# RWKV recurrence, Fourier mixing and MLP on one core: Fourier products folded twice along the features, a list scheduler with insertion, and key transposes by DMA

## The chip, the cores and the metric

The program runs on one core of a Trainium2 chip. Its engines are TensorE (PE, with its weight loads shown apart as PEld), VectorE (DVE), ScalarE (ACT), GpSimd (POOL) and SyncE (SP), each with a queue of its own that is worked through in order; 16 DMA engines move data for all of them. The metric is the device time of one execution in microseconds, lower is better. The three runs before the change took 211.9, 212.37 and 209.75 us (median 211.9).

## What is computed

The inputs r, k, v have the shape (4 batches, 8 heads, 768 steps, 48 features), w and u are (8, 48), and the MLP has weights of 384x1536 and 1536x384. All inputs and the output are float32.

```
for t in range(S):                       # per batch and head, state is 48x48
    y[t]  = r[t] @ (state + (u*k[t]) v[t]^T)
    state = w[:,None]*state + k[t] v[t]^T
x = y with the heads side by side        # (4, 768, 384)
u  = x + real(fft(fft(x, axis=1), axis=2))
un = (u - mean(u)) / sqrt(var(u) + 1e-6) # over the 384 features
out = u + relu(un @ w_ch1) @ w_ch2
```

## The kernel before

**Attention.** Each batch is cut into six chunks of 128 steps, 24 chunks in all (index i; q = i mod 6). For each chunk SP loads k, r (tile `kr`) and v (`vt`), lines 295 to 301. DVE scales k and r by powers of the decay into `KR` (L317), ACT casts v into `V` (L322), PE turns KR in eight 128x128 transposes (`tp`, L327), ACT copies the result out of PSUM (`KRT`, L330), PE multiplies keys and queries (`A_ps`, L341), and two masks give `MA` (ACT copy L353 with a GpSimd select L355, or one DVE multiplication, L348). PE also updates the state (`u_ps`, L369 and L372, DVE copy L376), multiplies queries and state (L396), and sums the masked rows into `yd` (L411). The bonus term u goes its own way: DVE forms `PR` (L331), PE sums it over the features (L391), ACT copies 8 numbers per step (`DE`, L401), GpSimd scales V by them (`TT`, L402), and DVE adds that to `yd` while it writes `X` (L415).

**Fourier part.** Per batch, `fold` (L425) adds and subtracts the two halves of the sequence (`EO`, L433), then the two halves of the features (`XF`, L439). `first` (L457) multiplies by cosine and sine tables over 384 steps: per batch 6 groups of three matmuls of 386 or 384 columns (L463), copied out by ACT (`TT2`, printed as TT, L470). `rev` (L478) copies it backwards into `TR` for the second half of the steps. `second` (L487) multiplies along the features, for each of six blocks of 128 steps two matmuls of 384 columns and four of 192 (L498, L500, L502). DVE adds X (`UF`, L508), and takes mean and variance (L513, L515). Three operations on ACT and DVE give the inverse deviation (square root L524, reciprocal L526, L528), ACT writes the normalised `UN` (L533). `UN` is turned into `UNT` by PE and DVE for batch 0 (L554, L557) and by a DMA transpose on SP for the other batches (L545).

**MLP.** Each batch has two halves of 384 steps (hf 0 to 7). For each half, 12 groups of three matmuls of 384 columns with W1 (L582), a rectifier on ACT (`HT`, L586), and for three blocks of 128 steps 12 matmuls with W2 (L598). DVE adds UF (`osb`, L605), and GpSimd issues the store (L608). W1 and W2 are loaded by six DMAs that GpSimd issues (L638), W1 once the fourth chunk's TT has been issued, W2 once the eighth's has.

**Order.** All work is handed to `_Schedule` (L74) as operations with an estimated duration, what they read and write, and a priority. `order` (L100) goes through time: it takes, over all engines, the operation that can start first, ties by priority, and never puts an operation ahead of one that it has placed. PSUM is divided by name: two banks for A_ps, one each for tp, u_ps and yd, and a ring of three (named "mm") for all Fourier and MLP products. Matmuls of zeros (L614) fill PE's idle time up to an estimated 46 us.

## Time and profile before

| | before |
|---|---|
| runs | 211.9, 212.37, 209.75 us |
| profiled execution, its own time | 211.41 us |
| its span | 209.7 us |
| mean granted TensorE clock | 0.958 |
| busy: PE, DVE, ACT, POOL | 186.7, 136.0, 129.5, 64.0 us |
| HBM read, written | 20.32 MB, 4.72 MB |

The profile covers one execution. The span is the time between the first and the last instruction on the core; the execution's own time is 1.7 us longer. Busy time of PE counts matmuls from start to modelled end, and consecutive ones overlap, so what a stream of matmuls costs is read from the distance between their starts. Views used below: the page (shares and 40 slices), groups of instructions by line, the timeline (start, duration, instruction, and in brackets the idle time ahead of it with what ended it), the chain that ended last (start, duration, piece), and tables by stretch.

### The profile page before, as it was taken

Reading aid. Unit: us, or ns where it says so; the run is one execution under the profiler, and the core shown is the slowest. Engines: PE = TensorE matmul, PEld = TensorE weight load, DVE = VectorE, ACT = ScalarE, POOL = GpSimd, SP = SyncE. Lnnn points to the kernel's source line nnn. Section 1 sums busy time; section 2 is a strip of 40 time slices with the busy share of each in tenths; the row PEclk is TensorE's granted clock in tenths of the full one; section 3 lists DMA queues with packets and bytes.
Section 4 is the critical chain, followed back from the end, with each engine's and each line's share of the span. In section 5 each row is a group of like instructions: output and inputs, shape, how many; then the busy total and the mean of one; then the engine's idle time right before and its main releaser. Section 6 shows DMA issues by size and latency. Waiting matters only on the chain.

```text
span 209.7 us, 4438 instructions
## 1 busy us (share of the span) xinstructions
PE 186.7 (89%) x1729; PEld 118.7 (57%) x1731; DVE 136.0 (65%) x281; ACT 129.5 (62%) x260; POOL 64.0 (31%) x92
## 2 busy tenths in 40 slices
PE   7199975599999699999789999999999999999990
PEld 2056643267576366577457567666567665666550
DVE  5178999649999448899897999883739511111221
ACT  3467852562898686874678986987371895364300
POOL 5017793111038244442344323234110121121131
PEclk9969998569999999999969999999999999999999
DMA  5999999999759999967567000044110144112122
GB/s 103 181 188 190 258 219 210 182 191 172 125 106 164 193 179 219 219 131 150 113 144 150 12 3 0 30 104 94 41 38 0 42 99 126 38 41 75 38 75 75
DMA packets 86548, 24.73 MB, mean 118 GB/s; under 512 B 82944, under 2 KB 84608, under 8 KB 86528
## 3 DMA queue, kind: packets, MB, share of 16 engines
q1 hardware_dynamic: 82848, 17.37, 47.4%
q0 software_dynamic: 3680, 7.08, 13.3%
q8 instruction: 13, 0.21, 0.5%
q14 instruction: 7, 0.06, 0.1%
HBM read 20.32 MB, written 4.72 MB: 119 GB/s over the span
## 4 chain that ended last, share of the span: by engine, by line
PE 37%; issue 27%; DVE 11%; DMA 11%; POOL 6%; ACT 3%; SPq 2%; POOLq 0%; ACTq 0%; DVEq 0%
PE mm L598 7%; DMA vt<-in_v_dram 6%; PE mm L582 5%; DMA kr<-in_r_dram 5%; PE mm L614 4%; PE tp L327 4%; POOL out_dram L608 4%; PE mm L463 3%; DVE KR L317 3%; PE mm L498 3%; PE A_ps L341 2%; PE u_ps L369 2%; DVE XF L439 2%; DVE X L415 1%; PE yd_ps L411 1%
## 5 line engine op out<-in xcount | busy, mean ns | idle before, releaser
L586 ACT ACTIVATE HT<-mm 128x384 bf16<-128x384 f32 x96 | 45.9, 493 | 22.5 <-PE mm L582 22.1
L582 PE MATMUL mm<-UNT,W 128*128 128x384 bf16 x288 | 53.7, 330 | 0.5 <-DVE osb L605 0.3
L598 PE MATMUL mm<-W,HT 128*128 128x384 bf16 x288 | 51.1, 326 | 0.0
L605 DVE TENSOR_TENSOR osb<-mm,UF 128x384 f32<-128x384 f32 x24 | 13.3, 555 | 37.9 <-PE mm L598 37.9
L598 PEld LDWEIGHTS <-HT 128*128 128x128 bf16 x288 | 27.7, 98 | 17.6
L582 PEld LDWEIGHTS <-W 128*128 128x128 bf16 x288 | 27.3, 99 | 17.5 <-issue 1.4
L355 POOL TENSOR_SCALAR_AFFINE_SELECT MA<-AC 128x512 bf16<-128x512 bf16 x29 | 19.4, 676 | 50.4 <-ACT AC L353 49.3
L402 POOL TENSOR_TENSOR TT<-V,DE 128x384 bf16<-128x384 bf16 x24 | 25.0, 1040 | 27.7 <-ACT DE L401 27.0
L608 POOL DMA_DIRECT2D out_dram<-osb x24 | 13.3, 554 | 62.6 <-DVE osb L605 57.6
L317 DVE TENSOR_TENSOR KR<-kr,wtab 128x768 bf16<-128x768 f32 x24 | 24.9, 1044 | 8.6 <-ACT wtab L244 5.7
L330 ACT COPY KRT<-tp 128x1024 bf16<-128x1024 bf16 x24 | 24.5, 1019 | 6.2 <-PE tp L327 6.0
L353 ACT CAST AC<-A_ps 128x512 bf16<-128x512 f32 x29 | 16.6, 591 | 11.7 <-PE A_ps L341 11.7
L614 PE MATMUL mm<-zero 128*128 128x512 bf16 x71 | 20.1, 423 | 1.4 <-DVE wuc L233 1.3
L327 PE MATMUL tp<-ident,KR 128*128 128x128 bf16 x192 | 15.7, 229 | 5.8 <-DVE KR L317 5.6
L322 ACT CAST V<-vt 128x384 bf16<-128x384 f32 x24 | 12.0, 522 | 8.9 <-DMA vt<-in_v_dram 5.1
L327 PEld LDWEIGHTS <-KR 128*128 128x128 bf16 x192 | 12.4, 103 | 9.1 <-DVE KR L317 6.4
L533 ACT ACTIVATE UN<-UF,nm,rstd 128x384 bf16<-128x384 f32 x24 | 15.7, 699 | 2.8 <-DVE nm L528 2.8
L415 DVE TENSOR_TENSOR X<-yd_ps,TT 128x384 bf16<-128x384 f32 x24 | 13.1, 546 | 5.7 <-POOL TT L402 5.7
L470 ACT CAST TT<-mm 128x386 bf16<-128x386 f32 (+1 forms) x24 | 12.7, 600 | 4.3 <-PE mm L463 4.3
L331 DVE TENSOR_TENSOR PR<-KRT 128x512 bf16<-128x512 bf16 x24 | 14.1, 596 | 0.5 <-ACT KRT L330 0.4
L508 DVE TENSOR_TENSOR UF<-mm,X 128x384 f32<-128x384 f32 x24 | 12.7, 551 | 1.8 <-PE mm L502 1.1
L348 DVE TENSOR_TENSOR MA<-A_ps,mtri 128x512 bf16<-128x512 f32 x19 | 12.9, 681 | 1.1 <-PE A_ps L341 1.0
(67 smaller groups left out, 239.6 us busy)
## 6 DMA issues: line engine op xcount, KB each, us to landing
kr<-in_k_dram SPq DMA_DIRECT2D x24, 192.0 KB, 4.5
kr<-in_r_dram SPq DMA_DIRECT2D x24, 192.0 KB, 4.6
vt<-in_v_dram SPq DMA_DIRECT2D x24, 192.0 KB, 4.4
out_dram<-osb POOLq DMA_DIRECT2D x24, 192.0 KB, 2.2
W<-in_moe_w_ch_dram POOLq DMA_DIRECT2D x6, 384.0 KB, 7.7
hid_t<-hid_c SPq DMA_DIRECT2D x1, 576.0 KB, 5.1
te_t<-te_c SPq DMA_DIRECT2D x1, 289.5 KB, 4.3
to_t<-to_c SPq DMA_DIRECT2D x1, 288.0 KB, 4.0
```

Source lines behind the costliest of these rows:

```text
L317: op("DVE", 960, lambda: nc.vector.tensor_tensor(out=KR().rearrange("t s p (a d) -> t (s p) a d", a=2)[:, :, :, 0:D], in0=kr().rearrange(" ...
L327: nc.tensor.transpose(tp()[:, s, p, :], KR()[:, s, p, :], ident)
L330: op("ACT", 1010, lambda: nc.scalar.copy(KRT(), tp()), r=[("tp", i)], w=[("KRT", i)], new=[KRT], use=[tp], pri=pri)
L353: op("ACT", 590, lambda: nc.scalar.copy(AC(), A_ps[a]()), r=[("A", i)], w=[("AC", i, a)], new=[AC], use=[A_ps[a]], pri=pri)
L355: op("POOL", 680, lambda: nc.gpsimd.affine_select(out=MA[a](), in_=AC(), pattern=[[0, NP], [1, 128]], base=0, channel_multiplier=-1, compa ...
L402: op("POOL", 850, lambda: nc.gpsimd.tensor_tensor(out=TT(), in0=V(), in1=DE().unsqueeze(2).to_broadcast([128, H, D]), op=AluOp.mult), r=[( ...
L533: op("ACT", 705, lambda: nc.scalar.activation(out=UN()[:, j, :], in_=UF()[:, j, :], func=Act.Identity, scale=rstd()[:, j:j + 1], bias=nm() ...
L582: nc.tensor.matmul(hp(), lhsT=W1[:, dt, ft * 128:(ft + 1) * 128], rhs=UNT()[:, :, dt, :], start=(dt == 0), stop=(dt == 2))
L586: op("ACT", 490, lambda: nc.scalar.activation(out=HT()[:, ft, :], in_=hp(), func=Act.Relu), r=[("hp", hf, ft)], w=[("HT", hf, ft)], new=[H ...
L598: nc.tensor.matmul(mo(), lhsT=HT()[:, ft, j * 128:(j + 1) * 128], rhs=W2[:, ft, :], start=(ft == 0), stop=(ft == 11))
L608: op("POOL", 550, lambda: nc.gpsimd.dma_start(out=out[b, row:row + 128, :], in_=osb()), r=[("osb", hf, j)], w=[("out", hf, j)], use=[osb], ...
L614: op("PE", 216, lambda: nc.tensor.matmul(z(), lhsT=zero[:, 0:128], rhs=zero, start=True, stop=True), r=["zero"], w=[("idle", len(sch.ops)) ...
```

## The change

The mathematics of the Fourier part changes, and the order is made in another way.

- **Fourier tables and folds.** The features are folded a second time: after EO, `shift` writes the sum and difference of the feature halves into `XP` (192 features and a zero behind them), and `mirror` adds and subtracts XP and its reverse into `XF` (97 features used). `first` then has per batch four groups of six matmuls, each with 97 columns of weights and 193 columns of the table. `second` has four matmuls of 192 columns per block, with weights of 97 rows, and a fifth that adds X through the identity matrix (384 columns). ACT copies UF out of PSUM, and DVE takes the statistics from PSUM.
- **Inverse deviation** by logarithm and exponential on ACT (`exp(-0.5*ln(var+eps))`), so that one table of ACT functions is loaded, not two.
- **Attention.** The keys of chunks 12 to 23 are turned by a DMA transpose on SP straight into KRT. In chunks 0 to 5 PE adds TT to yd through the identity and ACT copies X. The bonus sums have a PSUM tile of their own. For every chunk one mask is made by DVE and one by ACT and GpSimd. PR reads one factor from PSUM for chunks 0 to 11.
- **Start and end.** The order of the constants is changed; the tables are loaded ahead of the sixth chunk's v; W1 and W2 are both issued behind the seventh chunk's TT. The first half of batch 0 is normalised and turned block by block, and its first MLP product is done by blocks of 128 steps (`block1`). Turned by PE: first halves of batch 0 and 3; the other six halves by DMA. The stores are issued by ACT.
- **Order.** `order` now takes groups of operations that share a PSUM tile, sorted by a number per kind of work (chunk index plus an offset from the table `SH`), and places each group at the first gap in which its engines, the DMA engines and the port shared by DVE and GpSimd are free. Every PSUM tile may take any of the eight banks.

```diff
-        t = np.concatenate([np.cos(a), np.sin(a)], axis=1)
+        t = np.zeros((384, 2, 193))
+        t[:, 0, :len(k)] = np.cos(a)
+        t[:, 1, :len(k)] = np.sin(a)
+OPT = dict(SH=dict(L=-1.45, K=0.25, P=2.3, U=2.85, A=2.1, D=-23.75, ...
+           MA0=lambda i: "D", XA=lambda i: i < 6, UFA=lambda b: True,
+           VC=lambda i: False, KT=lambda i: i >= 12, OUT="ACT",
+           G1=[("TT", 6)], G2=[("TT", 6)],
...
+        for o in sorted(self.ops, key=lambda o: (o["pri"][0] + OPT["SH"][o["pri"][1]], o["n"])):
...
+                free = [b for b in banks if b.free(s, e - s) == s]
...
+        if OPT["KT"](i):
+            op("SP", 1500, lambda: nc.sync.dma_start_transpose(
+                out=KRT().rearrange("c s p t -> c (s p) t"), in_=KR().rearrange("t s p c -> t (s p c)")),
+               r=[("KR", i)], w=[("KRT", i)], new=[KRT], use=[KR], dma=1400, pri=at["K"])
...
+        if xa:
+            op("PE", 165, add, r=[("TT", i), ("y", i)], w=[("ya", i)], use=[yd, TT], pri=at["Y"])
+            op("ACT", 540, lambda: nc.scalar.copy(X()[:, q, :], yd()), r=[("ya", i)], ...
...
+        def mirror(h, alu):
...
+            nc.vector.tensor_tensor(out=dst, in0=src[nd + (slice(0, 98),)], in1=src[nd + (slice(192, 94, -1),)], op=alu)
...
-                nc.tensor.matmul(fp(), lhsT=XF()[:, par, nb, cb * 128:(cb + 1) * 128], rhs=tab[:, nb, :],
-                                 start=(nb == 0), stop=(nb == 2))
+                nc.tensor.matmul(fp()[:, par, :], lhsT=XF()[:, h, par, nb, a, 0:97],
+                                 rhs=(te_t, to_t)[par][:, nb, 193 * trig:193 * trig + 193],
+                                 start=(par == 0 and nb == 0), stop=(par == 1 and nb == 2), skip_group_check=True)
...
+                for g in range(4):
+                    nc.tensor.matmul(mp()[:, g % 2, :], lhsT=src()[0:97, g, lo:lo + 128],
+                                     rhs=hid_t[0:97, g + (2 if sh and g > 1 else 0), :], start=(g == 0),
+                                     stop=(g == 3 and not OPT["UFA"](b)), skip_group_check=True)
+                if OPT["UFA"](b):
+                    nc.tensor.matmul(mp(), lhsT=ident, rhs=X()[:, blk, :].rearrange("p (m a) -> p a m", a=2), start=False,
+                                     stop=True, skip_group_check=True)
...
+                    nc.scalar.activation(out=rstd()[:, j0:j1], in_=MV()[:, j0:j1, 1], func=Act.Ln, bias=eps_t[:, 0:1])
+                    nc.scalar.activation(out=rstd()[:, j0:j1], in_=rstd()[:, j0:j1], func=Act.Exp, scale=-0.5)
...
-    weights("W1", lambda n: w1[n * 128:(n + 1) * 128, :], lambda n: W1[:, n, :], [("TT", 3)])
+    weights("W1", lambda n: w1[n * 128:(n + 1) * 128, :], lambda n: W1[:, n, :], OPT["G1"], 2300)
```

How the order moves, at three places.

GpSimd, around the loads of W1 and W2 (TT is the bonus term of one chunk, MA a mask). Before:

```order
L402 TENSOR_TENSOR TT_446<-V_292,DE_431 128x384
L355 AFFINE_SELECT MA_497<-AC_485 128x512
L355 AFFINE_SELECT MA_516<-AC_495 128x512
L402 TENSOR_TENSOR TT_527<-V_377,DE_512 128x384
L638 DMA W1_121<-in_moe_w_ch1_dram 128x1536 x3
L355 AFFINE_SELECT MA_608<-AC_567 128x512
```

With the change:

```order
L558 TENSOR_TENSOR TT_492<-V_459,DE_472 128x384
L515 AFFINE_SELECT MA_552<-AC_488 128x512
L515 AFFINE_SELECT MA_563<-AC_544 128x512
L558 TENSOR_TENSOR TT_597<-V_537,DE_533 128x384
L558 TENSOR_TENSOR TT_668<-V_617,DE_635 128x384
L856 DMA W1_94<-in_moe_w_ch1_dram 128x1536 x3
L856 DMA W2_95<-in_moe_w_ch2_dram 128x4x384 x3
L515 AFFINE_SELECT MA_743<-AC_644 128x512
```

W1 moves from behind the fourth chunk's TT to behind the seventh's, and W2 from four chunks later to right behind W1.

ACT, from the last chunk of batch 0 to the first normalised block of batch 0 (X is the attention result, KRT, V, DE and AC belong to the next chunks, TT2 and UF to the Fourier part). Before, from the chunk after batch 0 on:

```order
L322 CAST V_668<-vt_348 128x384
L330 COPY KRT_698<-tp_683 128x1024
L322 CAST V_704<-vt_412 128x384
L353 CAST AC_719<-A_ps_707 128x512
L470 CAST TT2_727<-mm_610 128x386
L470 CAST TT2_727<-mm_612 128x2x192
```

With the change:

```order
L486 COPY KRT_608<-bank0_96 128x1024
L447 CAST V_617<-vt_531 128x384
L557 COPY DE_635<-bank0_96 128x8
L583 CAST X_279<-bank1_97 128x384
L513 CAST AC_644<-bank2_98 128x512
L447 CAST V_653<-vt_594 128x384
L486 COPY KRT_678<-bank0_96 128x1024
L557 COPY DE_705<-bank0_96 128x8
L513 CAST AC_708<-bank3_99 128x512
L655 CAST TT2_718<-bank4_100 97x2x193
L447 CAST V_734<-vt_642 128x384
L691 COPY UF_750<-bank6_102 128x2x192
```

The last X of batch 0 is now on ACT, behind KRT, V and DE of the seventh chunk; the Fourier copies of batch 0 stand behind V of the eighth chunk, and UF behind V of the ninth.

SP, in the last batch (KRT is the new transpose of a chunk's keys, UNT that of a normalised half). With the change:

```order
L435 DMA kr_2030<-in_k_dram 128x8x48
L437 DMA kr_2030<-in_r_dram 128x8x48
L481 DMA_TRANSPOSE KRT_2054<-KR0_87 128x8x128
L445 DMA vt_2089<-in_v_dram 128x8x48
L435 DMA kr_2107<-in_k_dram 128x8x48
L437 DMA kr_2107<-in_r_dram 128x8x48
L445 DMA vt_2139<-in_v_dram 128x8x48
L748 DMA_TRANSPOSE UNT_2166<-UN_2124 128x9x128
L748 DMA_TRANSPOSE UNT_2233<-UN_2191 128x9x128
L481 DMA_TRANSPOSE KRT_2286<-KR1_88 128x8x128
```

Before, this queue held only loads there, and the transposes of UN behind them. Now a transpose of a chunk's keys stands among the loads of the chunks that follow it by one or two.

More of the change, by code (lines that the diff above doesn't have):

```diff
@@ new lines, in order, with warm @@
+        while groups:
+            for i, g in enumerate(groups):
+                if settle(g):
+                    del groups[i]
+                    break
+            else:
+                raise AssertionError("nothing can be placed")
+        self.lines, self.banks = lines, banks
+        return sorted(self.ops, key=lambda o: (o["start"], o["n"]))
+    def warm(self, fn, first, last, ns):
+        pe, made = self.lines["PE"], []
+        t = first
+        while t < last:
+            t = pe.free(t, ns)
+            if t >= last:
+                break
+            free = [i for i, b in enumerate(self.banks) if b.free(t, ns) == t]
+            if not free:
+                t += 50
+                continue
+            pe.take(t, t + ns)
+            self.banks[free[0]].take(t, t + ns)
+            made.append(dict(start=t, end=t + ns, eng="PE", n=-1, w=["idle"], pri=0, new=[], fn=lambda i=free[0]: fn(i)))
+            t += ns
+        return made
@@ L275 @@
     sch = _Schedule()
+    banks = [ps.tile([128, 512], F32, name=f"bank{n}") for n in range(sch.BANKS)]
     op = sch.op
@@ L564, in fourier @@
             MV = new(wp, [128, 3, 2], F32, "MV", 3)
[L565 to L567 removed]
+            half(sh, UF, UNT, MV)
             bat[b]["halves"].append((UF, UNT))
```

740 lines of the change are left out of this document (440 added, 300 removed).

## The prediction

> **What bounds the kernel now.** I read the page first: which engine is busy, and when.
>
> ```profile
> PE 186.7 (89%) x1729; PEld 118.7 (57%) x1731; DVE 136.0 (65%) x281; ACT 129.5 (62%) x260; POOL 64.0 (31%) x92
> PE   7199975599999699999789999999999999999990
> PEclk9969998569999999999969999999999999999999
> ```
>
> PE is at nine tenths in most slices, but busy time hides two things: in the first quarter it is partly matmuls of zeros, and its clock drops around slices 8 and 9. So I next asked when the MLP begins, with the tile view of UNT, and then how PE does from there, with the table by stretch.
>
> ```profile
> L582 PE MATMUL mm<-UNT,W x288: 322/326/527, 56.8 to 196.3; 128*128 128x384 bf16 x144
> 30.00:40.00 10.00, 5.73 (x62) 3.38 (x62) 9.28 (x19) 2.35 (x5) 3.02 (x4) 0.76 1.03 197
> 70.00:80.00 10.00, 7.93 (x86) 5.11 (x85) 4.40 (x8) 7.41 (x17) 2.82 (x3) 1.00 1.09 187
> 100.00:110.00 10.00, 7.91 (x76) 4.73 (x75) 9.29 (x23) 6.63 (x13) 3.82 (x6) 0.84 0.61 133
> 190.00:200.00 10.00, 10.00 (x63) 6.01 (x62) 1.67 (x3) 3.90 (x8) 1.62 (x3) 1.00 0.11 39
> ```
>
> (Columns: length, busy PE, PEld, DVE, ACT, POOL, granted clock, DMA share, GB/s.) The first MLP product starts at 56.8. From there PE works until the last store; only the stretches 70 to 80 and 100 to 110 show real gaps, 2.07 and 2.09 us, with about 1 us more in the others. The kernel therefore has two parts: a front of 56.8 us that is set by waits, and a rest in which PE's work is the time. A change helps by starting the MLP earlier or by taking PE work out of the rest.
>
> What holds up the front is in the timeline, here its rows for the last chunks of batch 0 and for what follows them:
>
> ```profile
> 18.54 0.97 SPq L297 DMA_DIRECT2D kr<-in_r_dram  x1
> 23.74 0.84 SPq L297 DMA_DIRECT2D kr<-in_r_dram  x1
> 27.45 1.69 POOL L638 DMA_DIRECT2D W<-in_moe_w_ch_dram  x3
> 34.20 1.58 DVE L317 TENSOR_TENSOR KR<-kr,wtab 128x768 bf16<-128x768 f32 x1
> 35.71 0.55 DVE L415 TENSOR_TENSOR X<-yd_ps,TT 128x384 bf16<-128x384 f32 x1
> 39.83 0.51 ACT L322 CAST V<-vt 128x384 bf16<-128x384 f32 x1 [1.90 <-DMA vt<-in_v_dram]
> 46.22 0.33 PE L498 MATMUL mm<-hid_t,TT 128*128 128x384 bf16 x1
> ```
>
> The last X of batch 0 is written at 35.7. Then ACT stands until 39.8 for a v that SP loaded while W1 was also in flight, the second Fourier product starts at 46.2 and the MLP ten microseconds later, after all six blocks of the batch have gone through DVE.
>
> **The change, part one: when the MLP starts.** Two things must meet, the first normalised block and W1. Landing times, from the DMA part of the page and the tile view of W (least, median, most):
>
> ```profile
> kr<-in_r_dram SPq DMA_DIRECT2D x24, 192.0 KB, 4.6
> W<-in_moe_w_ch_dram POOLq DMA_DIRECT2D x6, 384.0 KB, 7.7
> DMA to landing us min/median/max: 5.8/7.7/10.0
> UNT<-UN SPq DMA_TRANSPOSE x6, 3.2
> ```
>
> The chain of a chunk and of a block comes from these groups of the page and of its long form:
>
> ```profile
> L330 ACT COPY KRT<-tp 128x1024 bf16<-128x1024 bf16 x24 | 24.5, 1019 | 6.2 <-PE tp L327 6.0
> L470 ACT CAST TT<-mm 128x386 bf16<-128x386 f32 (+1 forms) x24 | 12.7, 600 | 4.3 <-PE mm L463 4.3
> L533 ACT ACTIVATE UN<-UF,nm,rstd 128x384 bf16<-128x384 f32 x24 | 15.7, 699 | 2.8 <-DVE nm L528 2.8
> L439 DVE TENSOR_TENSOR XF<-EO 128x384 bf16<-128x384 bf16 (+1 forms) x12 | 8.6, 747 | 0.2
> ```
>
> In the new ACT order the last X of batch 0 stands behind KRT, V and DE of the seventh chunk. That chunk's r was issued at 23.74 and lands 4.6 later, 28.3; the load order up to there carries about the same bytes, so I keep it. KR (1.0, the uncontended part of its 1.58), the eight transposes 0.45, KRT 1.02, V 0.5, PR and DE 0.6, X 0.55, and some 0.6 for eight handovers make 33.0, against 35.71 + 0.55 = 36.3 now. From there: three pairs of folds on DVE at about 0.7 a pair, 2.1; the eighth chunk's KRT and PR, which stand between the pairs in DVE's order, 1.5; eight matmuls 0.7; two copies out 1.2 (ACT and DVE share the four); one block of the second product 0.5, statistics 0.75, inverse and its product 0.65, UN 0.7, turning and copying 0.55, handovers 1.0. That is 9.7, so the first block is ready at 42.7. It needs no other block, where now all six pass first.
>
> W1 now leaves GpSimd behind the seventh chunk's TT, which waits for the same DE as above: about 33.5. Now it is issued at 27.45, its third part at about 28.6, and with the most, 10.0, it is there at 38.6, 11.1 after the first issue. So W1 lands at 44.6, and **the MLP starts at 44.6, 12.2 us earlier.** W1, not the chain, decides. Ends: 40 if each part takes the least (33.5 + 1.1 + 5.8), 53 if the three share the DMA engines with W2 and the loads so that they take twice as long (33.5 + 2 x 10).
>
> **Part two: PE's work after that.** Counts in the rest (groups of PE from 56.7 on, the last row a weight load from the groups of the whole span), then paces (pieces of the chain, and starts in the timeline):
>
> ```profile
> L327 PE MATMUL tp<-ident,KR 128*128 128x128 bf16 x120 | 9.2, 220 | 0.1
> L463 PE MATMUL mm<-te_t,XF 128*128 128x386 bf16 x27 | 6.1, 327 | 0.0
> L463 PE MATMUL mm<-to_t,XF 128*128 128x384 bf16 x27 | 5.9, 325 | 0.0
> L498 PE MATMUL mm<-hid_t,TT 128*128 128x384 bf16 x18 | 5.9, 326 | 0.0
> L500 PE MATMUL mm<-hid_t,TT 128*128 128x192 bf16 x18 | 4.4, 246 | 0.0
> L500 PEld LDWEIGHTS <-TT 128*128 128x128 bf16 x24 | 2.3, 98 | 0.3
> ```
>
> ```profile
> 77.39 1.95 PE mm L598 x12
> 81.13 0.45 PE tp L327 x8
> 121.57 1.48 PE mm L463 x9
> ```
>
> ```profile
> 156.44 0.33 PE L498 MATMUL mm<-hid_t,TT 128*128 128x384 bf16 x1
> 156.60 0.25 PE L500 MATMUL mm<-hid_t,TT 128*128 128x192 bf16 x1
> 156.68 0.25 PE L502 MATMUL mm<-hid_t,TT 128*128 128x192 bf16 x1
> 156.76 0.33 PE L498 MATMUL mm<-hid_t,TT 128*128 128x384 bf16 x1
> ```
>
> So 384 columns cost 0.163, 192 cost 0.082, a transpose 0.056.
> - Key transposes: 120 now, 32 with the change (four chunks): 88 x 0.056 = 4.9 less.
> - First product: 54 x 0.164 = 8.9 now; 72 of 193 columns at 0.083 = 6.0: 2.9 less.
> - Second product: 36 of 384 and 72 of 192 (the rows above, L502 like L500, and as many for TR) = 11.8 now; 72 x 0.082 and 18 identity matmuls x 0.163 = 8.8: 3.0 less.
> - The rest of the new order, one chunk's scores, one state update, the first MLP half in blocks of 128 columns: 0.9 more.
>
> **Together 9.9 us less.** Nothing in the trace has weights of 97 columns; every load there has 128 and is hidden, as the 0.082 between matmuls of 192 shows. I take it as hidden; if the 98 ns of a load were added whole, 72 x 0.098 = 7.1 would come back.
>
> The Trainium skill speaks against the change here: "TensorE: Matmul & The Clock Gate", section on weight-path performance modes, says that fast weight loads are on only when the number of weights is 128. By its formula for a plain load, columns over 1.2, 97 columns take 81 ns, an estimate; hidden behind a matmul of 193 columns that costs nothing, unhidden 5.8 us. No run so far shows such a load.
>
> **Part three: what moves to others.** The 12 transposes by DMA also spare ACT 12 x 1.02 us, and take (by the UNT row) 3.2 us each to land, against 0.45 + 1.02 now. They wait on SP for DVE's KR; behind them stand the loads of the chunk after next, for which V on ACT and KR on DVE wait. Cover is the MLP work between a chunk's KR and its scores; without it each costs 3.2 - 1.5 = 1.7, 20 in all. ACT gains UF (24 copies like L470's, at most 0.6) and the stores:
>
> ```profile
> L295 SPq DMA_DIRECT2D kr<-in_k_dram x24: 367/862/3478, 1.3 to 111.3; - x24
> L586 ACT ACTIVATE HT<-mm 128x384 bf16<-128x384 f32 x96 | 45.9, 493 | 22.5 <-PE mm L582 22.1
> ```
>
> An issue takes 0.37 when the queue is free, so 24 stores hold ACT for 9 us. After 44.6 ACT has the rectifiers (45.9 us), 21 UN at 0.7 (15), about 65 copies of V, masks, Fourier results and UF at 0.5 to 0.6 (36), stores 9, and small ones 7: 113 of about 137 us. It keeps up if its order is right. The doubled folds on DVE, six pairs where there were four operations of 0.75, cost 1.5 per batch (3 if the backward reads halve their speed), behind MLP work. Inverse, table load and free banks change PE's time only through waits.
>
> **The waits left.** PE has 5.2 us of gaps after 60 now. Eight free banks and an order with look-ahead should close part of them. New is W2: behind W1 it lands 11 later, at 55.6; PE needs it after three blocks of W1 products and two chunks' attention, about 8 us after 44.6, and so waits 3. I take the sum of waits as unchanged; ends: 5 less (all gaps closed), 12 more (W2, two late chunks, ACT behind).
>
> **The end** barely moves:
>
> ```profile
> 204.44 0.56 DVE L605 TENSOR_TENSOR osb<-mm,UF 128x384 f32<-128x384 f32 x1 [1.39 <-PE mm L598]
> 205.29 0.54 POOL L608 DMA_DIRECT2D out_dram<-osb  x1 [1.41 <-DVE osb L605]
> ```
>
> ACT instead of GpSimd issues the last store in 0.37 instead of 0.54: 0.2 less.
>
> **Sum:** span 209.7 - 12.2 - 9.9 + 0 - 0.2 = 187.4; the profiled execution took 1.7 more than its span, so 189.1, and I say **189.0 us**. That execution took 211.41, the median of the three runs is 211.9, so no correction is needed. A change of 2% is 4.2 us, about what measurements of this kernel can tell from none.
>
> **Rivals.**
> - *W1 late* (0.14). The six weight DMAs share the DMA engines with the loads, as at 30 to 40, where v came late; the MLP starts at 53. For it: W2 is issued right behind. Against: W2 is behind W1 in the same queue. 189 + 8 = 197.
> - *97-column weight loads not hidden* (0.10). 189 + 7.1 = 196. This is the skill's rule in its worst form; all its loads with 128 columns are hidden, which speaks for neither side.
> - *Better* (0.12). Loads of W1 near the least and the gaps closed: 189 - 4.6 - 5 = 179. For it: order with look-ahead. Against: the DMA engines are busier than now.
> - *SP's queue becomes a loop* (0.03), the slower end. If every key transpose holds up the loads that its own next chunk needs, a chunk takes two issues and the landing of r, 1 + 4.6, KR 1.0, the transpose 3.2 and v's issue 1.0, 10.8 us in all. There are about 85 us from the 13th chunk to the last, 7.1 for each; beyond that it decides. 189 + 12 x 3.7 = 233. Against: in the new SP order the loads of one or two later chunks stand ahead of each transpose, so two or three chunks are in flight.
> - *The order does not do what it says* (0.03): its durations are off, queues block each other, and the front stays as it is. Only the PE work is saved: 211.4 - 9.9 = 201.5.
>
> **Chances.** The forecast, 183 to 195, has 0.58. Its bounds and the nearer rivals give a range of **178 to 200**, which leaves out the last two and the far ends. Faster by over 2% (under 207.7): 0.94; within 2%: 0.03; slower: 0.03.
>
> **What would show it.** First MLP product at 42 to 47, W1's last landing just ahead of it. Distances of 0.083 between matmuls with 97 columns of weights. 96 key transposes on PE, 12 on SP landing in 3 to 4 us. PE gaps after the start of 3 to 8 us in sum, the largest before the first W2 product. PE at nine tenths in every slice from there to the end. I am wrong if the MLP starts after 50, if the first product's matmuls are 0.15 or more apart, or if PE waits for KRT or V in the later batches.

## The result, and the profile after

The changed kernel took 197.17 us (median of four runs, 196.71 to 199.37), the kernel before 210.82 (209.07 to 212.37) beside it: a ratio of 0.938, interval 0.9288 to 0.9472. The forecast was 189.0, so the sign and the range held and the likeliest number was 8.2 us too low. The profiled execution took 197.39, its span is 195.7 (209.7 before).

The experiments below ran on four chips; times are medians, and spans, starts and waits are those of the profiled execution, in which PE sometimes lost its clock for a few microseconds (in e2, e3, e4, e7, e8, e10, e11 and e12, where it is said).

First the page of the changed kernel, the busy times and the rows of PE and its clock, then the stretches that were shown of before:

```profile
PE 179.1 (92%) x1735; PEld 114.7 (59%) x1735; DVE 127.4 (65%) x261; ACT 125.9 (64%) x271; POOL 47.0 (24%) x65
PE   7998998858969999999999998999999998999993
PEclk9999999999999999999999999999999999999998
```

```profile
30.00:40.00 10.00, 8.04 (x96) 4.65 (x94) 8.02 (x17) 4.78 (x10) 6.37 (x10) 1.00 1.00 186
70.00:80.00 10.00, 9.55 (x104) 5.88 (x103) 9.47 (x14) 7.88 (x19) 2.96 (x4) 1.00 0.78 174
```

PE's clock is at nine tenths or more in every slice but the last, and from 70 to 80 PE is busy for 9.55 of 10 us, where it was for 7.93. Now the start of the MLP, from the tile view of W:

```profile
L800 PE MATMUL bank<-UNT,W x108: 216/219/219, 51.4 to 64.8; 128*128 128x128 bf16 x108
L856 POOL DMA_DIRECT2D W<-in_moe_w_ch_dram x6: 548/688/790, 35.8 to 38.9; - x6
DMA to landing us min/median/max: 5.0/8.7/11.7
```

The first MLP product starts at 51.4 (56.8 before; 44.6 was forecast). The three DMAs of W1 were issued at 35.76, 36.35 and 36.91, and by their semaphores the last landed at 44.9. **W1 was there 6.4 us ahead of the first product.** What came late is in the timeline of the front:

```profile
1.32 8.54 PE L836 MATMUL bank<-zero 128*128 128x512 bf16 x26 [1.32 <-DVE icol L383]
34.65 0.48 ACT L583 CAST X<-bank 128x384 bf16<-128x384 f32 x1
34.76 1.28 DVE L623 TENSOR_TENSOR XF<-XP 128x392 bf16<-128x392 bf16 x2
35.96 0.94 DVE L463 TENSOR_TENSOR KR<-kr,wtab 128x768 bf16<-128x768 f32 x1
36.83 0.68 DVE L508 TENSOR_TENSOR MA<-bank,mtri 128x512 bf16<-128x512 f32 x1
39.65 0.70 POOL L515 TENSOR_SCALAR_AFFINE_SELECT MA<-AC 128x512 bf16<-128x512 bf16 x1
39.75 2.47 DVE L623 TENSOR_TENSOR XF<-XP 128x392 bf16<-128x392 bf16 x2
40.25 0.88 POOL L558 TENSOR_TENSOR TT<-V,DE 128x384 bf16<-128x384 bf16 x1
41.04 0.68 POOL L515 TENSOR_SCALAR_AFFINE_SELECT MA<-AC 128x512 bf16<-128x512 bf16 x1
44.40 0.50 ACT L691 COPY UF<-bank 128x384 f32<-128x384 f32 x1 [0.52 <-PE bank L685]
44.93 0.57 DVE L694 BATCH_NORM_STATS2 st<-bank 128x6 f32<-128x384 f32 x1 [0.82 <-ACT UF L691]
47.65 0.36 DVE L760 COPY UNT<-bank 128x384 bf16<-128x384 bf16 x1 [0.42 <-PE bank L757]
50.86 0.33 PE L757 MATMUL bank<-ident,UN 128*128 128x128 bf16 x3
```

Read it from the top. Matmuls of zeros hold PE to 9.86, so the first key transposes start at 9.70. The last X of batch 0 is cast at 34.65. Between the folds DVE runs KR (0.94) and a mask (0.68) of other chunks. The last two folds take 2.47, while GpSimd runs a mask, TT and a mask; the two before them took 1.28, the first pair of the batch (at 28.88) 0.65. The first block's UNT is ready at 48.01. The MLP product stands on PE behind the turns of all three blocks, of which the last runs at 50.86.

Matmuls of the first Fourier product, with 97 columns of weights, in the same timeline:

```profile
35.23 0.24 PE L644 MATMUL bank<-te_t,XF 128*97 128x193 bf16 x1
35.31 0.25 PE L644 MATMUL bank<-to_t,XF 128*97 128x193 bf16 x1
35.40 0.25 PE L644 MATMUL bank<-te_t,XF 128*97 128x193 bf16 x1
```

What PE does from its first MLP product on, in the long form of its groups from 51 us:

```profile
L644 PE MATMUL bank<-te_t,XF 128*97 128x193 bf16 x36 | 6.5, 251 | 1.0 <-DVE XF L623 0.9
L681 PE MATMUL bank<-hid_t,TT 97*128 97x192 bf16 x36 | 4.5, 245 | 0.0
L478 PE MATMUL bank<-ident,KR 128*128 128x128 bf16 x32 | 2.5, 220 | 1.5 <-DVE KR L463 1.5
```

Taking each line's median distance from start to start in the trace, times its count, gives PE's work after the start: 137.7 before, 126.9 after. With that the span falls into four parts:

| part, us | before | after | difference | forecast |
|---|---|---|---|---|
| start of the MLP | 56.8 | 51.4 | -5.4 | -12.2 |
| PE's work from there | 137.7 | 126.9 | -10.8 | -9.9 |
| what is left: waits | 9.6 | 13.7 | +4.1 | 0 |
| last product to the end | 5.6 | 3.7 | -1.8 | -0.2 |
| span | 209.7 | 195.7 | -14.0 | -22.3 |

A part of the 5.4 may be clock: before, the granted clock was half from 36 to 44, while PE ran the first products of batch 0 (their starts 0.3 us apart there, 0.16 at full clock); after, it was 1.00 from 30 to 50. No run separates this. Of the waits before, at most 1.7 (an estimate: half of 3.4 us) are clock too, as it was half from 106.8 to 110.3.

The waits are many and small. Three of PE's, summed over the whole span (in us, how many, the longest; the longest of the first, 1.6, stands ahead of the first MLP product):

```profile
PE bank L644 <- DVE XF L623: 2.9, 4, 1.6
PE bank L478 <- DVE KR L463: 1.8, 3, 1.0
PE bank L553 <- DVE PR L488: 1.3, 4, 0.3
```

Most end on DVE. The idle time that the trace has ahead of PE's matmuls from the first MLP product on is 6.1 us in 24 gaps, 5.2 in 8 before. The table has more, since a matmul in front of a gap counts as busy to its modelled end. The end of the program, where the store has moved to ACT (issued 0.03 behind the end of `osb`, in 0.34; before 0.29 behind it, in 0.54):

```profile
192.89 0.34 ACTq L831 DMA_DIRECT2D out_dram<-osb  x1
```

### The profile page after: what moved, and what is told of

Read it like the earlier page. It is cut to its first block, busy times and chain, and to the rows that moved or that the text cites. A ratio compares the mean times of both kernels' runs of the same rounds, so it can differ in the third digit from the quotient of the medians.

```text
span 195.7 us, 4458 instructions
## 1 busy us (share of the span) xinstructions
PE 179.1 (92%) x1735; PEld 114.7 (59%) x1735; DVE 127.4 (65%) x261; ACT 125.9 (64%) x271; POOL 47.0 (24%) x65
## 4 chain that ended last, share of the span: by engine, by line
PE 60%; DVE 22%; ACT 9%; issue 3%; DMA 2%; POOL 1%; POOLq 0%; ACTq 0%; DVEq 0%
PE bank L818 20%; PE bank L783 14%; PE bank L836 7%; ACT KRT L486 5%; DVE st L694 4%; PE bank L644 4%; DVE XF L623 3%; PE bank L478 3%; DMA UNT<-UN 2%; DVE XP L612 2%; DVE PR L488 2%; PE bank L501 2%; PE bank L800 2%; DVE EO L608 2%; DVE MV L704 2%
## 5 line engine op out<-in xcount | busy, mean ns | idle before, releaser
L818 PE MATMUL bank<-W,HT 128*128 128x384 bf16 x288 | 49.7, 326 | 0.0
L787 ACT ACTIVATE HT<-bank 128x384 bf16<-128x384 f32 x84 | 40.2, 492 | 11.0 <-PE bank L783 10.9
L783 PE MATMUL bank<-UNT,W 128*128 128x384 bf16 x252 | 44.5, 326 | 0.7 <-DMA UNT<-UN 0.4
L828 DVE TENSOR_TENSOR osb<-bank,UF 128x384 f32<-128x384 f32 x24 | 13.3, 556 | 34.1 <-PE bank L818 33.0
L836 PE MATMUL bank<-zero 128*128 128x512 bf16 x95 | 26.7, 413 | 1.9 <-DVE icol L383 1.3
L463 DVE TENSOR_TENSOR KR<-kr,wtab 128x768 bf16<-128x768 f32 (+1 forms) x25 | 24.5, 980 | 2.0 <-ACT wtab L393 1.5
L515 POOL TENSOR_SCALAR_AFFINE_SELECT MA<-AC 128x512 bf16<-128x512 bf16 x24 | 16.3, 678 | 37.7 <-ACT DE L557 24.8
L513 ACT CAST AC<-bank 128x512 bf16<-128x512 f32 x24 | 14.1, 591 | 12.3 <-DVE X L586 10.7
L486 ACT COPY KRT<-bank 128x1024 bf16<-128x1024 bf16 x12 | 12.1, 1011 | 9.5 <-PE bank L478 9.4
L508 DVE TENSOR_TENSOR MA<-bank,mtri 128x512 bf16<-128x512 f32 x24 | 16.4, 683 | 0.7 <-PE bank L501 0.7
L694 DVE BATCH_NORM_STATS2 st<-bank 128x6 f32<-128x384 f32 x24 | 13.0, 542 | 4.0 <-ACT UF L691 3.9
L447 ACT CAST V<-vt 128x384 bf16<-128x384 f32 x24 | 12.2, 519 | 2.3 <-DMA vt<-in_v_dram 2.3
```

The costliest lines, as they stand in the source:

```text
L463: nc.vector.tensor_tensor(out=KR()[:, s0:s1].rearrange("t s p (a d) -> t (s p) a d", a=2)[:, :, :, 0:D], in0=kr()[:, s0:s1].rearrange("t s ...
L486: op("ACT", 1010, lambda: nc.scalar.copy(KRT(), tp()), r=[("tp", i)], w=[("KRT", i)], new=[KRT], use=[tp], pri=at["K"])
L508: op("DVE", 680, lambda: nc.vector.tensor_tensor(out=MA[a](), in0=A_ps[a](), in1=mtri.unsqueeze(1).to_broadcast([128, NP, 128]), op=AluOp. ...
L515: op("POOL", 680, lambda: nc.gpsimd.affine_select(out=MA[a](), in_=AC(), pattern=[[0, NP], [1, 128]], base=0, channel_multiplier=-1, compa ...
L694: op("DVE", 550, lambda: nc.vector.bn_stats(out=st(), in_=mp().rearrange("p a m -> p (a m)")), r=[("mp", b, blk)], w=[("st", b, blk)], new ...
L783: nc.tensor.matmul(hp(), lhsT=W1[:, dt, ft * 128:(ft + 1) * 128], rhs=UNT()[:, :, dt, :], start=(dt == 0), stop=(dt == 2))
```

## The experiments

My theory after the result: the front is set by the order of the work and by what runs beside it, not by W1; the saving on PE is what was counted; and an early start is worth only the work that it takes out of the way. (The planner is `_Schedule` with `order`, its shifts are the fourteen offsets of the table `SH`, and its makespan is the time that it reckons for the whole program.) Rivals: W1 or the loads set the start; the smaller saving comes from the DMA turns or from ACT.

**e1_fillers: zeros at their true price.**

```diff
+            cost = ns * 1.9 if t < self.COLD else ns
-            t = pe.free(t, ns)
+            t = pe.free(t, cost)
...
-            made.append(dict(start=t, end=t + ns, eng="PE", ...
-            t += ns
+            made.append(dict(start=t, end=t + cost, eng="PE", ...
+            t += cost
```

> The planner prices a matmul of zeros at 0.216 us although its own rule prices PE work before 8 us at 1.9 times that; here the zeros before 8 us are priced at 0.41, so fewer of them stand ahead of the first key transposes. Theory (the front is set by the order of the work): the first key transposes start near 7.5 us instead of 9.70, every later chunk follows 3.2 us apart as before, the first MLP product comes 2 us earlier (49.4 for 51.36), time 195. Rival (the loads pace the chunks): the first transposes move, the later ones do not, start 51.4, time 197. Rival (fewer zeros cost clock): the granted clock falls below 0.9 somewhere ahead of 20 us, time 198 or more.

Measured: 196.09 us, 1.1 less than the changed kernel, and a span of 193.7, 2.0 less. The row of the zeros, and what follows it:

```profile
1.32 4.28 PE L837 MATMUL bank<-zero 128*128 128x512 bf16 x13 [1.32 <-DVE icol L384]
7.65 0.61 PE L479 MATMUL bank<-ident,KR 128*128 128x128 bf16 x8 [2.04 <-DMA ident<-id_c]
```

13 zeros instead of 26, the first transposes at 7.65 (they now wait for the identity's load), the next chunks 3.2 to 3.5 apart as before, the first MLP product at 49.30. The whole front moved by 2.06, and the span by 2.0. From the first transposes on the order sets the pace, not the loads, and the clock stayed at 1.00. The exact gain varies: with the same 26 zeros the first transposes began between 8.33 and 9.90 in the experiments that keep them (e2 to e5, e7), since the moment at which PE gets its full clock (the last zero at half pace between 4.2 and 7.3) varies.

**e2_w1_early: W1 seven microseconds earlier, the order otherwise kept.**

```diff
         order = self.order()
+        at = next(o["start"] for o in order if o["w"][0] == ("TT", 4))
+        for o in order:
+            if o["w"][0][0] == "W1":
+                o["start"] = at + 1
```

> W1's three transfers are issued behind GpSimd's TT of the fifth chunk instead of the seventh, about 7 us earlier; every engine's order is otherwise that of the changed kernel. Theory (the chain of folds, products and statistics decides the start, W1 is there in time): the first MLP product stays within 0.5 us of 51.36 or comes later by the time that the loads lose to W1, time 197 to 200. Rival, the prediction's own step (W1's landing decides): W1 lands near 38 and the first product comes at about 45, time 191.

Measured: 203.1, 202.6, 201.5 and one execution of 195.6 in which the clock held at 1.00. In the profiled one (span 201.4) W1 was there at 36.9, twenty microseconds ahead of the first product at 57.16. ACT's row shows why that came so late:

```profile
48.13 0.51 ACT L451 CAST V<-vt 128x384 bf16<-128x384 f32 x1 [4.28 <-DMA vt<-in_v_dram]
```

The load of v for the ninth chunk was issued at 37.48, among the weights, and landed 10.6 us later; the cast V stands on ACT ahead of UF, which follows at 48.54, and everything behind waits for UF. Then PE, idle, lost its clock (0.61 from 52 to 56). The execution of 195.6 is 1.1 us below the fastest of the changed kernel, not the 6 that the prediction's step would give; no trace shows when its v landed. The step "W1 decides the start" is refuted. That W1 does better behind the loads than among them is shown by this one trace alone.

**e3_keys_pe and e5_keys_pe_tuned: all keys turned on PE.**

```diff
-           VC=lambda i: False, KT=lambda i: i >= 12, OUT="ACT",
+           VC=lambda i: False, KT=lambda i: False, OUT="ACT",
```

> The keys of all 24 chunks are turned on PE and copied by ACT, none by DMA; the planner makes its order anew. Theory (the DMA turns take PE work away and bring no wait with them): 96 transposes of 0.056 us more on PE, 5.4 us, time 202.5. Rival (half of what they spare comes back as waits for KRT and DE): time 199. Rival (ACT's 12 more copies of 1.02 us make ACT late): time 206 or more.

Measured: 217.43, 20 us more than the changed kernel, which only the last rival (206 or more) allows. Since the planner's own makespan rose by 15, part of that had to be its fourteen shifts, which were fitted to other work. So in e5 they are fitted again (K 0.5, P 67.4, U 3.3, A 2.55, D -73.7, and so on):

> As e3_keys_pe (all keys turned on PE), but the fourteen shifts of the planner's priorities are fitted to this set of operations, by the planner's own makespan (200.6 us, where it gave 208.4 with the shifts of the changed kernel, and 193.2 for the changed kernel). Theory (most of e3's loss above PE's 5.9 us is an order that was fitted to other work): 204.5. Rival (turning by DMA is what keeps the chunks ahead; PE waits for the product of the keys whatever the order): 212 or more.

Measured: 206.91, span 205.0. Against the changed kernel PE's work after the start is 132.15 for 126.91 (+5.2, the 96 transposes), the waits 18.5 for 13.7 (+4.8), the start 1.0 earlier (0.7 of it because its first transposes began at 9.04). One of its waits:

```profile
PE bank L501 <- ACT KRT L486: 2.1, 5, 0.9
```

So ten of e3's twenty microseconds were a badly fitted order (with the clock that e3 lost, 0.984), five are PE's transposes, and five are more waits. Of these, 1.4 is PE's wait for KRT (2.1 where it was 0.7); the rest is not assigned, and two orders that were fitted apart differ in more than the turns. That the turns by DMA remove waits is therefore only in part shown; that they bring none with them fits both runs. The rival of a loop in SP's queue falls with it: each lands 2.7 to 5.1 after its issue.

**e4_old_fourier: the Fourier products of before in everything else that is new.** The tables, XF, TT2 and the products of before, priced as there:

```diff
-                    nc.tensor.matmul(mp()[:, g % 2, :], lhsT=src()[0:97, g, lo:lo + 128], ...
+                    nc.tensor.matmul(flat, lhsT=src()[:, 1, ri, lo:lo + 128], rhs=tb[:, 192:576], ...
+                    nc.tensor.matmul(flat[:, 0:192], lhsT=src()[:, 0, ri, lo:lo + 128], ...
+                    nc.tensor.matmul(flat[:, 192:384], lhsT=src()[:, 2, ri, lo:lo + 128], ...
```

> The Fourier products of the kernel before (one fold of the features, 384 and 192 columns, 128 columns of weights) in the changed kernel with its new planner, its DMA turns and the residual on TensorE. Theory (the fold is worth its PE work): first product 2.9 us more, second product 36 x 0.163 + 72 x 0.082 - 72 x 0.082 = 5.9 us more, in the front one pair of folds less and two copies more that cancel: time 206. Rival (the small waits that the changed kernel has come from the doubled folds and vanish with them, 4 us): time 202. Rival (nearly all comes from the planner): time 199 or less.

Measured: 206.44 (205.01 to 208.48), 9.3 above the changed kernel. PE's work after the start is 135.69, 8.8 more, as summed. The start is 48.9, 2.5 earlier: the last fold of batch 0 is over at 37.7, in the changed kernel at 42.2, and no mask or TT of GpSimd runs beside it. The waits are 2.9 more, but the granted clock was half from 53.9 to 57.3 and from 170.0 to 173.4, and each of these stretches costs up to 1.7 us (an estimate: half of 3.4). So the saving of 8.8 on PE is shown. The 9.3 of time is not the fold's alone: without the lost clock about 6 would be left, since the longer chain of folds takes back 2.5 at the start. The rival that the small waits come from the doubled folds falls, as they are no fewer here.

**e6_port_free: GpSimd's masks behind the last folds** (with the zeros of e1).

```diff
+            def keep():
+                if i == 6:
+                    nc.gpsimd.tensor_copy(probe, bat[0]["XF"]()[0:1, 1, 1, 2, 1, 0:2])
+                nc.gpsimd.affine_select(
...
+            op("POOL", 680, keep, r=[("AC", i, a)] + ([("XF", 0, 2, 1)] if i == 6 else []), ...
```

> e1_fillers with one more operation: ahead of the first mask of the seventh chunk GpSimd copies two elements of the last folded part of batch 0, so its mask, TT and mask, which ran at the same time as DVE's last two folds, come behind them. Theory (GpSimd's work stretches the folds): the pair takes 0.75 us instead of 2.48, the first MLP product comes 1.7 us earlier than in e1 (47.6 for 49.30), span 192.0 for 193.7. Rival (the backward reads of the fold are slow by themselves): the pair stays above 1.5, span 193.7 or more. Rival (X of the eighth chunk gets late in turn): start earlier, span 193.7 or more.

Measured: 194.39 us (194.03 to 195.05), span 192.3. The folds on DVE, and GpSimd behind them:

```profile
38.39 0.64 DVE L630 TENSOR_TENSOR XF<-XP 128x392 bf16<-128x392 bf16 x2
```

```profile
39.10 0.18 POOL L519 COPY probe<-XF 1x2 bf16<-1x2 bf16 x1 [0.76 <-DVE XF L630]
39.23 0.63 POOL L520 TENSOR_SCALAR_AFFINE_SELECT MA<-AC 128x512 bf16<-128x512 bf16 x1
```

The pair takes 0.64 instead of 2.48 in e1 (2.47 in the changed kernel). From the eighth chunk's transposes to the first MLP product are 12.47 us (35.71 to 48.18), in e1 14.29 (35.01 to 49.30): 1.8 less, as expected. The span gained 1.4, since here the first transposes, which wait for the identity's load, began 0.7 later than in e1. This is the fastest kernel of the study, 1.4% below the median of the changed one (on another chip), and a ratio of 0.9304 (0.9225 to 0.9383) to the kernel before, whose own times there spread from 208.2 to 217.5.

**e7_ufa_off: the residual on DVE again** (`UFA=lambda b: False`, shifts fitted anew).

> The residual is added on DVE as in the kernel before (no identity matmul, no copy by ACT; statistics read UF), with the planner's shifts fitted to it (its own makespan is 197.9, for 193.2 with the residual on TensorE). Theory (DVE's 24 additions of 0.55 us are paid by waits that outweigh PE's 18 x 0.163 = 2.9 us): time 200 to 202. Rival (after the start only PE's work counts): 194.3. Rival (equal, since the statistics wait for ACT's copy of the same bank anyway): 197.

Measured: 200.9 (199.53 to 201.35), 3.7 more than the changed kernel, although PE has 18 matmuls of 0.175 less. The direction is the theory's, the size is not shown: in the profiled execution (span 199.6, 3.9 more) the granted clock was half from 58.4 to 61.8 and from 96.0 to 99.4, up to 1.7 us each (an estimate: half of 3.4). Without them some 0.5 is left, which the last rival, equal, allows as well. That the additions' waits made PE lose its clock is possible and was not tested.

**e8_block_first and e9_block_port: an earlier first product.** One group of 12 products is moved on PE, on top of e1 and of e6:

```diff
         order = self.order()
+        o = next(o for o in order if o["w"][0] == ("hp", 0, 0, 0))
+        o["start"] = next(p for p in order if p["w"][0] == ("UNT", 0, 0, 0))["end"] + 80
+        for t in o["new"]:
+            if t.ring is None:
+                t.slot = 3
```

> e1_fillers with one group of 12 MLP products (0.69 us) of the first block moved on PE from behind the turns of all three blocks to right behind the first UNT copy, in a bank that is free then; nothing else moves. Theory (the start by itself is worth nothing, only the work that is moved out of the way counts): the first MLP product comes at 46.0 for 49.30, the span falls by 0.7 to 193.0. Rival (the start counts in full, as the prediction's sum has it): span 190.4. Rival (W1 is not yet there or the other work is pushed back): span 193.7 or more.

Measured: first product at 47.44, 1.9 earlier, and a span of 195.5, 1.8 longer than e1. The rows from the last folds on show something that e1 did not have:

```profile
40.12 0.29 PE L650 MATMUL bank<-te_t,XF 128*97 128x193 bf16 x1 [1.63 <-DVE XF L629]
```

```profile
40.00:42.00 2.00, 1.88 (x11) 1.17 (x12) 1.55 (x5) 1.47 (x3) 0.00 (x0) 0.70 1.07 209
42.00:44.00 2.00, 2.00 (x11) 1.38 (x10) 0.23 (x1) 0.29 (x2) 0.00 (x0) 0.50 1.23 197
```

PE stood for XF, as in e1, but here the clock fell to half from 40.8 to 44.2, which costs up to 1.7. The move could not be judged, so I repeated it without that stall:

> e8_block_first on top of e6_port_free instead of e1_fillers, so that the stall of the last folds, after which the clock fell in e8, is gone. Theory (an early start is worth only the work that it takes out of the way): the first MLP product about 3 us earlier than in e6 (45 for 48.18), the span 0.7 less than in e6, 191.6. Rival (the start counts in full, as the prediction's sum has it): span 189. Rival (PE, waiting at the moved products without matmuls of zeros behind it, loses its clock again): granted clock 0.5 to 0.7 for some us behind the first turn, span 193 or more.

Measured: the clock held, the first product started at 44.82, 3.4 earlier than in e6, **and the span was 193.9, 1.6 longer.** PE's rows:

```profile
44.82 0.28 PE L812 MATMUL bank<-UNT,W 128*128 128x128 bf16 x2
45.29 0.73 PE L812 MATMUL bank<-UNT,W 128*128 128x128 bf16 x10 [0.20 <-DMA W<-in_moe_w_ch_dram]
45.86 1.24 PE L848 MATMUL bank<-zero 128*128 128x512 bf16 x5
46.94 0.33 PE L769 MATMUL bank<-ident,UN 128*128 128x128 bf16 x3
52.49 0.62 PE L485 MATMUL bank<-ident,KR 128*128 128x128 bf16 x8 [1.59 <-DVE KR L470]
```

After two products PE waits for W1's third part (it landed at 45.2), then the zeros that the planner had put there still run, and the second block is turned at 46.94 instead of 46.00. That 0.94 goes through UN, statistics and X to KR of the ninth chunk: its transposes start at 52.49 for 51.55. So neither the theory nor the first rival held: the early group gained nothing, because the next chain, not PE's work, still decides for some microseconds behind the start, and the group itself put that chain back. The 0.94 accounts for part of the 1.6; the rest, and what the move would be worth without that delay, stay open.

**e10_out_pool: the stores on GpSimd again** (e6 with `OUT="POOL"`).

> e6_port_free with the stores issued by GpSimd again instead of ACT (the planner prices it at 0.55 instead of 0.1 us and makes its order anew; its makespan rises by 1.5). Theory (the end of the program is 1.6 us longer behind a store of GpSimd: 0.3 of handover, 0.3 of landing, 1.3 from landing to the end): from the last product to the end 5.4 us instead of 3.7, span 194 for 192.3. Rival (the prediction: 0.2 of difference): 192.5. Rival (GpSimd relieves ACT by 24 issues of 0.34 us, 8 us, in which PE waited for ACT): 191 or less.

```profile
195.64 0.54 POOL L838 DMA_DIRECT2D out_dram<-osb  x1 [1.41 <-DVE osb L835]
```

Measured: from the last product to the end 5.6 (3.7 in e6), as the theory has it: 0.3 more until the issue, a landing of 2.2 instead of 1.9, and 1.3 more from the landing to the end. The time, 201.3, rose by more than that: waits of 19.2 for 13.5, of which some 3 are a stretch at half clock from 132 to 139. How much of the rest is the planner's new order was not separated.

**e11_refit: a planner that knows of the shared bank** (statistics and copy one after the other, other prices, shifts and choices fitted to the makespan).

> The changed kernel with the zeros priced as in e1, and with a planner that knows that ACT's copy UF and DVE's statistics of one bank come one after the other; loads and weights are priced at 1.02 and 2.0 us; fourteen shifts, the gate of the weights (two chunks earlier is allowed), the engine of twelve masks and of four copies are fitted anew to its makespan (189.9; the changed kernel's own plan said 193.2 and ran in 193.7 once the zeros were priced). Theory (what is left above PE's work are waits that a truer plan removes): span 190.5, time 192. Rival (the plan does not see GpSimd's and DVE's contention, and with twelve more masks on GpSimd DVE gets slower): span 194 to 198. Rival (a gap of PE costs it its clock): granted clock below 0.98, span 195 or more.

Measured: 193.81 in one execution, 198.05 to 199.01 in three with a clock of 0.974. The profiled one (span 197.3) belongs to these; ACT's row and PE's:

```profile
51.41 0.51 ACT L448 CAST V<-vt 128x384 bf16<-128x384 f32 x1 [10.23 <-DMA vt<-in_v_dram]
```

```profile
52.97 0.80 PE L682 MATMUL bank<-hid_t,TR 97*128 97x192 bf16 x4 [9.14 <-DVE st L700]
```

Again a v that was issued behind the weights: at 33.38, landed at 51.38, 18.0 later. PE stood for 9.1 us and then ran at half clock for five (granted 0.50 from 52 to 56). Behind the start its waits are 9.5 (13.7 in the changed kernel), but that start is at 59.2, and whether the truer plan or the late start makes them fewer was not separated. Not settled as a whole; the late v repeats what e2 showed.

**e12_kr_early: KR of the ninth chunk ahead on DVE** (e6 with one `start` changed to behind the third `nm` of batch 0, the factor that shifts a block by its mean).

> e6_port_free with one operation moved on DVE: KR of the ninth chunk, for which PE stood 1.02 us at 51.55, now stands behind the first statistics of the second half (from about 47.4), where DVE has 0.4 us free, instead of behind X of the seventh chunk. Theory (behind the MLP's start PE still waits for DVE's order, and what is moved out of the way counts there): the key transposes of the ninth chunk start at 50.6 for 51.55, those of the tenth at 52.4 for 53.02, the span falls by 0.6 to 191.7. Rival (the statistics and X of the seventh chunk are late in turn): span 192.3 or more. Rival (the next wait takes it all back): transposes earlier, span 192.3.

Measured: 195.54 (194.36 to 196.12), best span 192.7. In the profiled execution the first two chunks met a dip of the clock, which put its whole front 1.2 later, so I count from the first MLP product (49.38; 48.18 in e6). The transposes of the ninth chunk come 2.18 behind it (3.37 in e6), those of the tenth 4.08 (4.84), those of the eleventh 13.96 (13.83). PE's rows, e12 and then e6:

```profile
51.56 0.61 PE L482 MATMUL bank<-ident,KR 128*128 128x128 bf16 x8
53.46 0.62 PE L482 MATMUL bank<-ident,KR 128*128 128x128 bf16 x8 [0.49 <-DVE KR L467]
54.83 0.40 PE L505 MATMUL bank<-KRT 64*128 64x128 bf16 x8 [0.75 <-ACT KRT L490]
```

```profile
51.55 0.62 PE L480 MATMUL bank<-ident,KR 128*128 128x128 bf16 x8 [1.02 <-DVE KR L465]
53.02 0.62 PE L480 MATMUL bank<-ident,KR 128*128 128x128 bf16 x8 [0.48 <-DVE KR L465]
```

And ACT's of the same two:

```profile
51.98 1.91 ACT L737 ACTIVATE UN<-UF,nm,rstd 128x384 bf16<-128x384 f32 x3 [0.23 <-DVE nm L730]
53.79 0.99 ACT L490 COPY KRT<-bank 128x1024 bf16<-128x1024 bf16 x1
```

```profile
50.65 1.91 ACT L735 ACTIVATE UN<-UF,nm,rstd 128x384 bf16<-128x384 f32 x3 [0.23 <-DVE nm L728]
52.47 0.99 ACT L488 COPY KRT<-bank 128x1024 bf16<-128x1024 bf16 x1
```

The wait for KR (1.02) is gone and a wait for KRT (0.75) stands in its place. KRT stands on ACT behind the three UN of the second half, and these come 1.33 later than in e6, 0.1 more than the whole front does. The last rival holds: the next wait took it all back.

## Why the prediction was right, and where it was wrong

**What bounds the kernel: right in form.** A front set by waits and a rest in which PE's work is the time. Of the 14.0 us, 5.4 come from the front; the rest gives 10.8 in PE's work and 1.8 at the end, and loses 4.1 in waits.

**When the MLP starts: the step that failed.** The prediction said that W1 lands at 44.6 and decides, with the first block ready at 42.7. W1 landed at 44.9, which is luck: it was issued at 35.8 instead of 33.5 and took 9.2 instead of 11.1. It did not decide. The block was ready at 48.0 and the product came at 51.4; by its own test ("wrong if the MLP starts after 50") the step is wrong. By parts of its chain:
- The last X of batch 0: 33.0 forecast, 35.1 measured. I costed no zeros ahead of the first chunk; e1 shows 2.06 for them.
- From there to the last fold: 3.6 forecast (three pairs of folds and the eighth chunk's KRT and PR), 7.1 measured. I left out KR and a mask on DVE (0.94 + 0.68), and took a pair of folds at 0.7 although GpSimd works beside them; e6 shows 1.8 for that.
- From the last fold to UNT: 6.1 forecast, 5.8 measured.
- "It needs no other block": the planner put the product behind the turns of all three, 3.4 more. Taking this away gained nothing in e9, where the early group also put the next block back.

The last point is also an error of the sum: it took any earlier start as a term that counts in full. That holds when the whole front moves (e1: start 2.06 earlier, span 2.0 less; e6 against e1: 1.1 and 1.4). It did not where only the first group of products moved (e9: start 3.4 earlier, span 1.6 longer): up to where chunks nine and ten pass, PE still waits for DVE and ACT, as e9 and e12 show.

**PE's work: right.** First product 8.8 to 6.0 (-2.8; forecast -2.9), second product with the residual 11.7 to 9.1 (-2.7; -3.0), key transposes 6.7 to 1.8 (-4.9; -4.9), the rest -0.4 where 0.9 more was forecast. An identity matmul was put at 0.163 and costs 0.175. e4 confirms the Fourier part (8.8 summed, 8.8 measured).

**Weights of 97 columns: hidden.** Their load takes 124 ns where 128 columns take 97, as the long form of the weight loads of after shows:

```profile
L644 PEld LDWEIGHTS <-XF 128*97 128x97 bf16 x96 | 8.0, 124 | 5.6 <-DVE XF L623 5.4
L566 PEld LDWEIGHTS <-KRT 128*128 128x128 bf16 x80 | 5.4, 97 | 4.4 <-issue 2.1
```

Yet the matmuls start 0.083 apart, so the loads are behind them. The rival of 196 falls. The Trainium skill says in "TensorE: Matmul & The Clock Gate", section on weight-path perf modes, that fast weight loads are on when the number of weights is 128; the trace agrees in that the load of 97 columns is the slower one. By the same page's formula for a plain load, in its section on LDWEIGHTS, it would take 81 ns (an estimate); the trace has 124, and the trace decides.

**What moves to others: right about the DMA turns' landing (2.7 to 5.1, 3.2 forecast), perhaps too low about their worth.** The sum counted 4.9 for PE; e5 is 9.7 longer in all, 5.2 of it PE's work and 4.8 waits, which are not all shown to be the turns'.

**Waits: mis-sized.** 0 was forecast, 4.1 more came, inside the bounds. Counted as idle gaps of PE, as the prediction did, they are 6.1 for 5.2, inside its 3 to 8; most of the 4.1 is that there are 24 gaps instead of 8. The wait that I named, for W2, did not occur: W2 landed at 50.6 and its first product, at 60.9, did not wait. In its place came many short ones, mostly on DVE.

**The end: mis-sized.** -0.2 forecast, -1.8 measured. I took only the difference of the issue; e10 shows that GpSimd's store also lands later and ends later.

The sum of the misses: 6.8 at the start and 4.1 in waits, less 0.9 and 1.6 gained elsewhere, is 8.4, against a span 8.3 above the 187.4 of the sum. That the time still fell into the range is owed to PE's work, which was forecast for the right reason; the start missed by more than half.

## What to carry to other kernels

Follow a start to the operation that the product really stands behind in its queue, and list what other engines do beside each step of that chain, before naming the transfer that should decide. Before adding "starts earlier by x" to "less work by y", ask whether the whole front moves or only its first product: moving the whole front counted nearly in full here (e1, e6), moving only the first group of products gained nothing (e9). When a planner's shifts were fitted to one set of operations, undo a part only with the shifts fitted anew; here half of an apparent 20 us was the fit.

## What the runs showed of the hardware

- Two operations of DVE that read two bf16 tiles of SBUF took 0.65 us alone and 2.47 while GpSimd ran a mask, TT and a mask; the first of them ended 0.23 after GpSimd's last, so it waited for all three. This is as the Trainium skill has it in "SBUF — State Buffer", section "SBUF: two separate sides": the port pair that DVE and GpSimd share is an exclusive lock.
- PE's clock fell to half for 3.4 us behind a stall of only 1.63 us (e8, 40.8 to 44.2), and did not after an equal stall of 1.62 in the profiled execution of e1. In e7 it fell twice for 3.4 us (58.4 and 96.0), although no gap of PE behind the zeros of the start had been longer than 1.05 us. After 9.1 us (e11) it was half for five. The Trainium skill's "TensorE: Matmul & The Clock Gate", section on how the oscillation bites, draws the line at gaps of about 3.4 us; here shorter ones sufficed.
- A 192 KB load that was issued among the six weight loads of 384 KB each landed 10.6 (e2), 14.8 (e6) and 18.0 us (e11) later, where 3.6 was seen ahead of them. In e6 nothing waited for it.
- The statistics on DVE and the copy on ACT of one PSUM bank ran one after the other (44.40 to 44.90, then 44.93). The profile names ACT's copy as what released DVE, so the program keeps this order; what the bank itself would allow was not run.
